# A bias subtraction goes from VectorE to GpSimd, and one first-layer tile takes its low-weight products last

## The chip, the cores and the metric

The kernel runs on one core of one Trainium2 chip. The metric is the device time of one execution in microseconds. The kernel before takes 559.72 us (median of three runs, 559.51 to 559.85). A core has five engines that work side by side and meet through semaphores: TensorE (PE, matrix products), VectorE (DVE), ScalarE (ACT), GpSimd (POOL) and SyncE (SP), which here only issues transfers.

## The reference

The kernel normalises an input of 2048 rows and 512 columns, sends it through a long convolution (a state-space scan, done with Fourier transforms) and, beside that, through a two-layer network whose output gates the convolution:

```python
def _B_ref(x, w1, b1, w2, b2):
    h = jnp.einsum("bsd,df->bsf", x, w1) + b1
    h = _gelu(h)
    return jnp.einsum("bsf,fd->bsd", h, w2) + b2

x = A_u
xn = _layernorm(x, axis=-1)
s = _A_ref(xn, ...)            # convolution of xn with a kernel made from A, B, C
g = _silu(_B_ref(xn, B_w1, B_b1, B_w2, B_b2))
return x + s * g
```

All of it is float32. w1 is 512 x 1792, w2 is 1792 x 512, b2 has 512 entries. The change lies in the two-layer network, at its very beginning.

## The kernel before

**The split into high and low halves.** TensorE multiplies rounded numbers (type fp32r). To keep float32 accuracy every operand is held as two: a high half (the number rounded to fp32r) and a low half (the number less its high half). A product w·x is taken as wh·xh + wh·xl + wl·xh. For the weights, `split(f, k)` makes the four pieces of slice f: w1h and w2h by a cast on ScalarE (L239), w1l and w2l by a subtraction on VectorE or GpSimd (L241). For the input, `ln_high` (ScalarE, L378) and `ln_low` (VectorE, L384) make xh and xl from the transposed, normalised rows. Between the layers, ScalarE makes hf by the gelu (`gate`, L270) and its high half hh (`gate_high`, L276), and VectorE the low half hl (`ffn_rest`, L282).

**Tiles and slices.** The rows are taken in four tiles of 512; the hidden width of 1792 in 14 slices of 128. A step is one pair (v, f) of row tile and slice. In the first layer a step is 12 products of 128x512 into one PSUM bank: four pieces k of the 512 columns, three products each. There are two such banks (tag f1, bufs=2), so the first products of slice f wait until the gelu of slice f-2 has read its bank. `first_start` (L266) makes the first step with all wh·xh, then all wl·xh, then all wh·xl. `first_half(v, f, h)` makes all later steps in two calls, h = 0 for k = 0, 1 and h = 1 for k = 2, 3; its three lines are L256 (wh·xh), L257 (wh·xl) and L258 (wl·xh). `second_part` (L295 to L297, with the bias product of L294) makes the second layer for 128 rows.

**The bias row.** The bias b2 is added by a product too: a 128x512 tile b2r, zero but for row 0 (the high half of b2) and row 32 (the low half), is multiplied by a tile of ones (L294). `bias_load` brings b2 into rows 0 and 32 of a zeroed tile, `bias_high` casts it to b2r on ScalarE (L420), and `bias_low` (L423) then makes row 32 the difference: one instruction on a single partition with 512 columns.

**The order.** Every engine executes its own queue in the order in which the program issues the instructions; the order is written out by hand. `prologue()` comes first: the loads of the first two pairs of input tiles, weights of slices 0 and 1, the time-step arithmetic on GpSimd (L468 to L482), the parameters of the convolution kernel, then

```python
        bias_high()
        ln_stats(0, mv[:, 0:2, :])
        bias_low()
        ln_stats(1, mv[:, 2:4, :])
        split(0, 0)
```

and the normalisation, the transposes and `first_start`. `ln_stats` are the batch statistics on VectorE (L327, L328); the two calls take the first and the second pair of input tiles. After that a list of tokens sets the order. Its start is

```
WS.0.3 LD.0 LD.1 WS.1.0 WS.1.1 P.0 P.0 W.2 G.0 H.0 WB.2 P.0 WS.1.2 P.0 F.1.0 P.0 LS.3.1 LS.2.0 R.0 S.0.0
W.3 WS.2.0 LS.3.0 WS.2.1 LL.4 WS.1.3 LL.5 S.0.1 LS.2.1 WS.2.2 F.1.1 WB.3 F.2.0 ...
```

F.1.0 and F.1.1 are the two calls of `first_half` for step 1, which is (v, f) = (0, 1); S.0.0 and S.0.1 between them are the second layer of step 0 for its first 256 rows; R.0 makes hl of step 0; WS.1.2 makes w1l of slice 1. W and WB load a slice's weights over SyncE's queue into four staging buffers, so the load of slice f waits until slice f-2 has been split. P.0 are pieces of the parameters of the convolution kernel, among them six products on GpSimd (L496 to L501), two absolute values on ScalarE (L504, L505), and a chain on VectorE that starts at L508.

Of the kernel before, what the change touches and what calls it, by code (L numbers as in the profile page):

```python
# [24 lines left out]
KD = D // P  # L25
# [147 lines left out]
def kernel(  # L173
# [5 lines left out]
    V, A, GP, PE, SY = nc.vector, nc.scalar, nc.gpsimd, nc.tensor, nc.sync  # L179
# [69 lines left out]
    def first_half(v, f, h):  # L249
        xh, xl = xt[v]  # L250
        wh, wl, _, _ = W[f]
        if h == 0:
            pt[v, f] = ps1.tile([P, TB * P], F32, tag="f1", name=f"f1_{v}_{f}", bufs=2)
        p = pt[v, f]
        for k in (2 * h, 2 * h + 1):
            PE.matmul(p, wh[:, k, :], xh[:, k, :], start=(k == 0), stop=False)  # L256
            PE.matmul(p, wh[:, k, :], xl[:, k, :], start=False, stop=False)  # L257
            PE.matmul(p, wl[:, k, :], xh[:, k, :], start=False, stop=(k == KD - 1))  # L258
# [42 lines left out]
    SB = {}  # L301
# [118 lines left out]
        A.copy(b2r, SB["b2"])  # L420

    def bias_low():
        V.tensor_sub(b2r[32:33], SB["b2"][32:33], b2r[32:33])  # L423

    def bias_spread():
        SY.dma_start(b2b, b2.rearrange("(o d) -> o d", o=1).to_broadcast([P, D]))
# [242 lines left out]
    b2r = wka.tile([P, D], F32R, name="b2r")  # L669
# [7 lines left out]
    def prologue():  # L677
# [20 lines left out]
# [5 lines that stand above are left out]
# [26 lines left out]
    def skip_load():  # L729
# [3 lines left out]

    acts = {
        "F": lambda j, h: first_half(*steps[j], h),
        "G": lambda j: gate(*steps[j]),
        "H": lambda j: gate_high(*steps[j]),
# [357 lines left out]
    with tc.manual_schedule():  # L1095
# [9 lines left out]
        for p in "S0 F00 S1 S2 F01 S3 L0 F10 L1 A0 F11 A1 L2 L3 A2 A3".split():  # L1105
            if p[0] == "F":
                k = int(p[1]), int(p[2])
# [67 lines left out]
```

## Time and profile before

| | |
|---|---|
| time, median of 3 runs | 559.72 us (559.51 to 559.85) |
| the profiled execution's own time | 559.77 us |
| its span, first to last instruction | 558.0 us |
| TensorE busy | 540.2 us, 97% |
| VectorE busy | 454.2 us, 81% |
| ScalarE busy | 407.8 us, 73% |
| GpSimd busy | 296.3 us, 53% |
| mean granted TensorE clock | 0.998 |

Times in the profile are microseconds from the span's start. In a row of the timeline stand start, length, engine, line, operation, written tile, read tiles, and shapes; a bracket at its end tells how long the engine stood idle before it and what ended that. "PE" is TensorE's products; "SPq" is SyncE issuing a transfer. A row of a table of stretches has the stretch, its length, then the busy time of PE, PEld (weight loads of TensorE), DVE, ACT and POOL with counts, the granted clock, the transfer engines' mean share, and GB/s. Rows that sum up a line give the number, and the shortest, median and longest length in ns.

### The profile page before, as it was taken

Reading aid. Unit: us, or ns where it says so; the run is one execution under the profiler, and the core shown is the slowest. Engines: PE = TensorE matmul, PEld = TensorE weight load, DVE = VectorE, ACT = ScalarE, POOL = GpSimd, SP = SyncE. Lnnn points to the kernel's source line nnn. Section 1 sums busy time; section 2 is a strip of 40 time slices with the busy share of each in tenths; the row PEclk is TensorE's granted clock in tenths of the full one; section 3 lists DMA queues with packets and bytes.
Section 4 is the critical chain, followed back from the end, with each engine's and each line's share of the span. In section 5 each row is a group of like instructions: output and inputs, shape, how many; then the busy total and the mean of one; then the engine's idle time right before and its main releaser. Section 6 shows DMA issues by size and latency. Waiting matters only on the chain.

```text
span 558.0 us, 17143 instructions
## 1 busy us (share of the span) xinstructions
PE 540.2 (97%) x7179; PEld 432.1 (77%) x7179; DVE 454.2 (81%) x697; ACT 407.8 (73%) x602; POOL 296.3 (53%) x403
## 2 busy tenths in 40 slices
PE   8899999999999999999999999999999999999995
PEld 7567777777777777767777777777889998988872
DVE  6899999999997799988988969877357657767874
ACT  3589997977598999668989798995355565564542
POOL 5639585776966769857718747540320305014323
PEclk9999999999999999999999999999999999999999
DMA  8959337267468392426167049205965583615945
GB/s 188 288 161 311 84 96 210 61 210 228 135 189 269 133 295 81 143 75 192 57 188 219 21 114 186 61 11 181 365 245 79 140 128 95 191 46 127 197 120 113
DMA packets 108345, 86.92 MB, mean 156 GB/s; under 512 B 44294, under 2 KB 87562, under 8 KB 108268
## 3 DMA queue, kind: packets, MB, share of 16 engines
q1 hardware_dynamic: 97584, 65.37, 43.8%
q0 software_dynamic: 9568, 19.93, 12.1%
q8 instruction: 56, 0.92, 0.7%
q10 hardware_dynamic: 1116, 0.53, 0.4%
q14 instruction: 21, 0.17, 0.1%
HBM read 52.25 MB, written 33.55 MB: 154 GB/s over the span
## 4 chain that ended last, share of the span: by engine, by line
PE 68%; DVE 16%; issue 6%; DMA 5%; SPq 2%; ACT 1%; POOL 1%; DVEq 0%; POOLq 0%
PE z L295 8%; PE z L296 7%; PE z L297 7%; PE f L256 7%; PE f L258 7%; PE f L257 7%; PE s L883 6%; PE kg L656 5%; PE s L864 4%; PE sa L918 3%; DMA w2s<-in_B_w_dram 2%; PE ph L595 2%; PE w L936 2%; DVE e L641 2%; DVE hl L282 2%
## 5 line engine op out<-in xcount | busy, mean ns | idle before, releaser
L618 POOL TENSOR_TENSOR mm<-mm,rc 128x32 f32<-128x32 f32 (+4 forms) x150 | 110.7, 738 | 11.8
L295 PE MATMUL z<-w2h,hh 128*128 128x512 f32 x224 | 97.9, 437 | 0.0
L256 PE MATMUL f<-xh,w1h 128*128 128x512 f32 x220 | 92.0, 418 | 0.5 <-ACT hf L270 0.5
L297 PE MATMUL z<-w2h,hl 128*128 128x512 f32 x224 | 88.5, 395 | 0.9 <-DVE hl L282 0.9
L296 PE MATMUL z<-w2l,hh 128*128 128x512 f32 x224 | 88.7, 396 | 0.0
L258 PE MATMUL f<-xh,w1l 128*128 128x512 f32 x220 | 86.9, 395 | 1.5 <-DVE w1l L241 1.5
L257 PE MATMUL f<-xl,w1h 128*128 128x512 f32 x220 | 86.7, 394 | 0.0
L883 PE MATMUL s<-X,mc 64*64 64x128 f32 x2048 | 63.5, 272 | 0.9 <-issue 0.9
L900 DVE TENSOR_TENSOR t<-s,uh 128x512 f32<-128x512 f32 x64 | 41.1, 685 | 25.9 <-ACT uh L891 25.6
L883 PEld LDWEIGHTS s<-X,mc 64*64 64x64 f32 x2048 | 56.0, 133 | 4.8 <-issue 2.7
L641 DVE TENSOR_TENSOR e<-mm,ra 128x1024 f32<-128x1024 f32 x32 | 47.8, 1495 | 4.7 <-POOL mm L618 3.2
L297 PEld LDWEIGHTS z<-w2h,hl 128*128 128x128 f32 x224 | 42.1, 188 | 11.7 <-DVE hl L282 1.8
L258 PEld LDWEIGHTS f<-xh,w1l 128*128 128x128 f32 x220 | 41.3, 188 | 11.9 <-DVE w1l L241 2.1
L615 POOL COPY mm<-rc 128x32 f32<-128x32 f32 x30 | 15.4, 512 | 65.4 <-DVE e L648 49.0
L256 PEld LDWEIGHTS f<-xh,w1h 128*128 128x128 f32 x220 | 41.5, 189 | 10.3 <-ACT hf L270 1.2
L282 DVE TENSOR_TENSOR hl<-hf,hh 128x512 fp32r<-128x512 f32 x56 | 46.7, 838 | 3.4 <-ACT hh L276 3.3
L295 PEld LDWEIGHTS z<-w2h,hh 128*128 128x128 f32 x224 | 42.5, 190 | 9.0
L609 DVE SCALAR_TENSOR_TENSOR ra<-ra,ph 128x512 f32<-128x512 f32 x64 | 43.6, 681 | 6.9 <-ACT ra L603 6.0
L296 PEld LDWEIGHTS z<-w2l,hh 128*128 128x128 f32 x224 | 42.3, 189 | 7.9
L257 PEld LDWEIGHTS f<-xl,w1h 128*128 128x128 f32 x220 | 41.4, 188 | 8.9
L870 ACT COPY X<-s 128x512 f32<-128x512 f32 x56 | 28.9, 598 | 25.6 <-PE s L864 25.6
L645 DVE TENSOR_TENSOR e<-mm,ra 128x1024 f32<-128x1024 f32 x32 | 45.6, 1425 | 0.0
(185 smaller groups left out, 1146.2 us busy)
## 6 DMA issues: line engine op xcount, KB each, us to landing
x<-in_A_u_dram SPq DMA_DIRECT2D x16, 256.0 KB
xs<-x SPq DMA_DIRECT2D x16, 256.0 KB
xt_h<-xh POOLq DMA_DIRECT2D x4, 1024.0 KB, 5.4
xt_l<-xl POOLq DMA_DIRECT2D x4, 1024.0 KB, 7.3
kgd<-ko SPq DMA_DIRECT2D x32, 128.0 KB
za<-zo SPq DMA_DIRECT2D x4, 1024.0 KB
xh<-xt_h POOLq DMA_DIRECT2D x4, 1024.0 KB, 6.8
xl<-xt_l POOLq DMA_DIRECT2D x4, 1024.0 KB, 10.1
```

What stands on the lines that cost most here:

```text
L256: PE.matmul(p, wh[:, k, :], xh[:, k, :], start=(k == 0), stop=False)
L257: PE.matmul(p, wh[:, k, :], xl[:, k, :], start=False, stop=False)
L258: PE.matmul(p, wl[:, k, :], xh[:, k, :], start=False, stop=(k == KD - 1))
L282: V.tensor_sub(hl, hf, hh)
L295: PE.matmul(z, hh[:, s], wh, start=(f0 == 0 and not rows), stop=False)
L296: PE.matmul(z, hh[:, s], wl, start=False, stop=False)
L297: PE.matmul(z, hl[:, s], wh, start=False, stop=(f0 == FA - 1))
L609: V.scalar_tensor_tensor(ra[:, 0, c], ra[:, 1, c], MAGIC, p, op0=ALU.subtract, op1=ALU.subtract)
L618: GP.tensor_mul(mv[:, :, 0:3:2, w:2 * w], mv[:, :, 0:3:2, 0:w], rc[:, 2 + 2 * i:4 + 2 * i, :].rearrange("p j c -> p c j").unsqueeze(3).to_ ...
L641: V.tensor_mul(e1, m1.unsqueeze(1).to_broadcast([P, 2, CH, N1]), ra[:, :, :, :N1])
L645: V.tensor_mul(e2[:, :, :, :H], m2[:, :, :H].unsqueeze(1).to_broadcast([P, 2, CH, H]), ra[:, :, :, dn])
L883: PE.matmul(p[ka * 64:(ka + 1) * 64, r, o, :, jj], mc[h, k, ((0, 2), (1, 0))[c][o], :], xf[b][h, c, :, k, :], start=(c == 0), stop=(c == 1 ...
```

## The change

Two edits. `bias_low` is issued on GpSimd's queue instead of VectorE's; there it stands behind the time-step arithmetic and ahead of the six parameter products. And in step (0, 1) `first_half` issues its twelve products in another order: the first call makes the four wh·xh and the four wh·xl, the second the four wl·xh. The number of products and all operands stay the same, as do all other steps.

```diff
@@ def first_half(v, f, h)
         p = pt[v, f]
+        if (v, f) == (0, 1):
+            for w, x in (((wl, xh),) if h else ((wh, xh), (wh, xl))):
+                for k in range(KD):
+                    PE.matmul(p, w[:, k, :], x[:, k, :], start=(w is wh and x is xh and k == 0), stop=(w is wl and k == KD - 1))
+            return
         for k in (2 * h, 2 * h + 1):
             PE.matmul(p, wh[:, k, :], xh[:, k, :], start=(k == 0), stop=False)
@@
     def bias_low():
-        V.tensor_sub(b2r[32:33], SB["b2"][32:33], b2r[32:33])
+        GP.tensor_sub(b2r[32:33], SB["b2"][32:33], b2r[32:33])
```

On TensorE's queue the eight products without w1l now stand before the seven products of S.0.0 and S.0.1, and the four with w1l behind them; before, six stood on either side, two of each six with w1l.

## The prediction

> **What bounds the kernel now.** I read the head of the page first, then the chain of waits over the first 36 us, then the timelines of VectorE, TensorE, GpSimd and ScalarE over the same stretch.
>
> ```profile
> span 558.0 us, 17143 instructions
> PE 540.2 (97%) x7179; PEld 432.1 (77%) x7179; DVE 454.2 (81%) x697; ACT 407.8 (73%) x602; POOL 296.3 (53%) x403
> q8 instruction: 56, 0.92, 0.7%
> ```
>
> TensorE is busy for 97% of the span, so only time in which it stands still, or work taken off it, can be won. The change touches the first 26 us alone. The chain of waits there (start, length, what) is this:
>
> ```profile
> 1.38 4.27 DMA x<-in_A_u_dram
> 7.49 0.43 DVE b2r L423
> ...
> 19.25 5.83 DMA w2s<-in_B_w_dram
> ...
> 26.48 6.76 DMA w2s<-in_B_w_dram
> ...
> 35.04 0.50 PE f L256
> ```
>
> The subtraction that moves (L423) is in the chain. But from 19.25 to 33.24 us the chain is two weight loads with 1.40 us of work between them (25.08 to 26.48). That is the main thing to see: after the two edits come two transfers. The next rows are TensorE's in order of time (start, length; the bracket is what it stood still for).
>
> ```profile
> 18.59 0.40 PE L257 MATMUL f<-xl,w1h 128*128 128x512 f32 x1
> 20.49 0.50 PE L258 MATMUL f<-xh,w1l 128*128 128x512 f32 x1 [1.51 <-DVE w1l L241]
> 22.70 0.51 PE L297 MATMUL z<-w2h,hl 128*128 128x512 f32 x1 [0.30 <-DVE hl L282]
> 25.14 0.39 PE L256 MATMUL f<-xh,w1h 128*128 128x512 f32 x1
> 25.61 0.40 PE L258 MATMUL f<-xh,w1l 128*128 128x512 f32 x1
> 29.69 0.51 PE L256 MATMUL f<-xh,w1h 128*128 128x512 f32 x1
> 34.02 0.50 PE L297 MATMUL z<-w2h,hl 128*128 128x512 f32 x1 [0.57 <-DVE hl L282]
> 35.04 0.50 PE L256 MATMUL f<-xh,w1h 128*128 128x512 f32 x1 [0.52 <-ACT hf L270]
> ```
>
> The two starts at 25.14 and 25.61 are two products apart, so a 128x512 product takes a step of 0.235 us. The wait of 1.51 us in the tile of slice 1 is what the new order goes for.
>
> **The change part by part: GpSimd takes the subtraction.** These are VectorE's rows:
>
> ```profile
> 7.49 0.68 DVE L423 TENSOR_TENSOR b2r<-b2st,b2r 1x512 fp32r<-1x512 f32 x1
> 8.20 0.69 DVE L327 BATCH_NORM_STATS2 bst<-x 128x6 f32<-128x512 f32 x1
> 17.58 0.28 DVE L508 TENSOR_TENSOR pr_ci<-pr_bi,pr_cr 128x128 f32<-128x128 f32 x1
> 19.75 0.68 DVE L241 TENSOR_TENSOR w1l<-w1s,w1h 128x512 fp32r<-128x512 f32 x1
> 21.98 0.66 DVE L282 TENSOR_TENSOR hl<-hf,hh 128x512 fp32r<-128x512 f32 x1
> 24.78 0.67 DVE L241 TENSOR_TENSOR w1l<-w1s,w1h 128x512 fp32r<-128x512 f32 x1
> ```
>
> From 7.49 to the statistics at 8.20 are 0.71 us. Without the subtraction the statistics could begin 0.71 us earlier, if the second pair of input tiles is there. I think it is not:
>
> ```profile
> 0.75 2.48 SPq L322 DMA_DIRECT2D x<-in_A_u_dram  x4
> 5.65:8.00 2.35, 2.35 (x20) 2.35 (x20) 2.15 (x5) 0.48 (x1) 1.75 (x8) 1.00 1.06 234
> ```
>
> Four loads of 256 KB were issued one behind the other, ahead of all weights. In the chain the second landed at 1.38 + 4.27 = 5.65. At 234 GB/s (the last number of the second row) the other two need 0.262 MB / 234 GB/s = 1.12 us each: 7.89 us. So the second pair's statistics begin at about 7.95 and not at 7.49. I take 0.25 us off VectorE's line, not 0.71; the bounds are 0 and 0.71. VectorE runs from there to 17.58 almost without a gap, so the transposes and the first tile come earlier by the same.
>
> On GpSimd the subtraction is queued behind the time-step arithmetic (last row at 11.42) and ahead of the parameter products (first row at 12.49):
>
> ```profile
> 11.42 0.20 POOL L482 TENSOR_TENSOR sm_dt<-sm_e,sm_k 128x4 f32<-128x4 f32 x1
> 12.49 0.68 POOL L496 TENSOR_TENSOR pr_wr<-pr_cr,pr_br 128x128 f32<-128x128 f32 x1 [0.87 <-DMA pr_br<-in_A_B_re_dram]
> 15.29 0.90 POOL L501 TENSOR_TENSOR pr_wi<-pr_wi,pr_m 128x128 f32<-128x128 f32 x1
> 16.55 0.30 ACT L505 ACTIVATE pr_cr<-pr_wi 128x128 f32<-128x128 f32 x1
> L241 POOL TENSOR_TENSOR w2l<-w2s,w2h x4: 1284/1301/1663, 34.5 to 239.8; 128x512 fp32r<-128x512 f32 x4
> L241 POOL TENSOR_TENSOR w1l<-w1s,w1h x2: 1563/1772/1982, 187.6 to 203.3; 128x512 fp32r<-128x512 f32 x2
> ```
>
> No row shows GpSimd on one partition. VectorE's 1x512 took 0.68 us, like its 128x512 of the same kind (0.68 at 19.75), so the time goes by the 512 columns, and GpSimd's 128x512 subtractions of 1.28 to 1.98 us (minimum and maximum of the two rows) are the nearest. I take 1.3 us: 11.7 to 13.0. It first fills the 0.87 us that GpSimd stood idle, and then pushes the six products by 13.0 - 12.49 = 0.5 us (0.3 to 1.2): they end at 16.7 instead of 15.29 + 0.90 = 16.19. Behind them stands ScalarE's absolute value L505 (0.30 us), and behind that VectorE's L508. VectorE now reaches L508 at 17.58 - 0.25 = 17.33, GpSimd and ScalarE are through at 16.7 + 0.30 = 17.0, a few hundredths for the hand-over aside: hidden. The cover is gone if the subtraction takes more than about 1.6 us; at 1.98 us L508 starts at 17.75, 0.17 us later than before. TensorE reads the bias row only after slice 1's products, long after 13.7 us.
>
> On that price the Trainium skill has a rule against the change: SBUF — State Buffer, Who interferes with whom, says that a VectorE instruction with two SBUF inputs and a GpSimd one that reads SBUF shut each other out for a whole instruction. By it the subtraction could wait for one such VectorE instruction of 0.68 us, which gives 1.3 + 0.68 = 1.98 us, the upper bound that the second GpSimd row gives already.
>
> **The new order in the tile of slice 1 (L256 to L258 of that tile alone).** TensorE's work stays the same, 12 products; what moves is which of them need w1l. Before the rows of the second layer (one bias product, then z) stood six products, two of them with w1l; now eight without it. They begin at 18.35 - 0.25 = 18.10 (18.59 less a step, less VectorE's gain), take 8 x 0.235 = 1.9 us, and three more products of the second layer follow: 20.7 us. So the wait of 1.51 us for w1l goes. What is late next is hl, 21.98 + 0.66 on VectorE: with 0.25 off it is 22.4, and TensorE goes on at 22.70 - 0.25 = 22.45. The waits of 1.51 and 0.30 us become one of about 1.75 us. Behind it stand eight products now, not ten, which is 0.47 us. At the end of slice 1 TensorE is ahead by 0.25 + 0.47 = 0.7 us (0.3 to 1.2): it could start slice 2 at 24.42 instead of 25.14.
>
> **What the transfers leave of that.** ScalarE's rows (the bracket is what it waited for):
>
> ```profile
> 23.94 0.62 ACT L239 CAST w1h<-w1s 128x512 fp32r<-128x512 f32 x1 [2.38 <-DMA w1s<-in_B_w_dram]
> 27.02 0.62 ACT L239 CAST w1h<-w1s 128x512 fp32r<-128x512 f32 x1 [1.30 <-DMA w1s<-in_B_w_dram]
> 28.95 0.69 ACT L270 ACTIVATE hf<-f,b1s 128x512 f32<-128x512 f32 x1
> 32.59 0.62 ACT L239 CAST w1h<-w1s 128x512 fp32r<-128x512 f32 x1 [2.29 <-DMA w1s<-in_B_w_dram]
> 25.00:30.00 5.00, 5.00 (x22) 3.69 (x21) 3.35 (x10) 3.54 (x5) 2.59 (x5) 1.00 1.05 232
> 31.00:32.50 1.50, 1.50 (x8) 1.23 (x7) 1.40 (x6) 0.00 (x0) 0.00 (x0) 1.00 0.12 40
> ```
>
> Slice 2's high half is cast at 23.94, when its load lands, and done at 24.56. Its low half follows on VectorE (24.58 to 25.25), so slice 2's third product starts near 25.3 instead of 25.61: 0.3 us are left of 0.7. Slice 3's tile (29.69) needs the bank that the activation at 28.95 frees at 29.64; that stands on ScalarE behind the cast at 27.02, again a load. There 0 is left. The same comes once more at 35.04: the activation that TensorE waits for there (0.52 us, ACT hf) is queued behind the cast at 32.59. The transfer engines' share is 1.05 over 25 to 30 us: they are never idle, so a load asked for a few tenths earlier waits in the same line. Only slice 4's load is asked for earlier, by at most 24.78 - 24.58 = 0.2 us, since VectorE's low half of slice 2 releases its buffer.
>
> The sum, against the profiled execution's own 559.77 us (558.0 and 1.8 around it): 0.7 us at slice 1, 0.3 at slice 2, 0 to 0.2 from 35.04 on. I take 0.1 us. The median of the runs is 559.72, 0.05 below the profiled run, so I forecast 559.6 us. A measurement of this kernel can tell about 0.2%, 1.1 us; this is no difference.
>
> **The rivals.** *The gain stays.* If loads of slices 2 to 4 landed earlier with TensorE, 0.7 us would remain (1.2 at the bound): 559.0, at best 558.5. Against it stands the transfer share of 1.05. It ends inside 0.2% unless all bounds fall together.
>
> *The stragglers go.* From 31.0 to 32.5 us the transfer share is 0.12, two engines of 16, while ScalarE waits for slice 4: one or two engines hold the last parts back. One cause can be seen:
>
> ```profile
> q8 instruction: 1, 0.02, 3.3%
> ```
>
> This is from the DMA queues between 20 and 22 us (packets, MB, share of 16 engines). One packet of queue 8 kept one engine for 0.033 x 16 x 2 us = 1.06 us. The page has 56 such packets, 0.92 MB, which is 64 bytes for each of TensorE's 2 x 7179 instructions: blocks of TensorE's own program. The block came as TensorE went on after its wait, so it should now come about 2 us earlier, at 18 to 19 us. If it then does not hold the weights back, slices 3 and 4 land 1 to 1.5 us sooner, the wait at 35.04 goes, and hl of slice 1 (34.02, less 0.25) decides: about 1.1 us, 558.6.
>
> *The stragglers grow* (the slower side). The same block, now earlier, falls among input loads instead of the result stores, and costs its engine again 1.06 us or more before slices 2 to 4, whose parts stand in that engine's line. From the point where slice 3 lands after 27.0 and slice 4 after 32.6, every microsecond passes through the activations to 29.69 and 35.04: 1.1 to 1.5 us, 560.9 to 561.2. Runtime: NRT & Kernel Launch, Instruction fetch mechanics, in the Trainium skill, calls the cost of such a block mostly hidden; by that neither straggler rival moves the time, and it would be 559.6. The row of 1.06 us on one engine speaks for a cost.
>
> *It doesn't do what it says.* If the second pair of inputs lands after 8.2 us, VectorE gains nothing; only the 0.47 us remain at slice 1, and 0 at 29.69: 559.7, the same forecast.
>
> **How the numbers follow.** The forecast, with the last rival and the gain that stays within 0.2%: 0.60. Stragglers go, or the gain stays in full: 0.21. Stragglers grow, or GpSimd's 1.98 us and they together: 0.19. The likeliest case alone gives 559.0 to 560.1. For 8 in 10 the range reaches to the others' ends: 558.5 to 560.9, which leaves out some of the slower tail.
>
> **What would show it.** In the changed kernel: no wait for w1l in slice 1; one wait for hl of 1.5 to 2.1 us; the second pair's statistics at 7.9 to 8.0; GpSimd's 1x512 of 1.3 us at 11.7; casts of slices 2, 3 and 4 still at 23.9, 27.0 and 32.6 within some tenths; slice 3 at 29.7 and slice 4's tile at 35.0. I am wrong if those casts move by over half a microsecond either way, or if TensorE's start at 35.04 holds and the end still moves.

## The result: slower by half a per cent, and the profile after

| | before | changed |
|---|---|---|
| median of 20 runs each, side by side | 560.25 us (558.77 to 563.27) | 563.72 us (559.66 to 565.34) |
| ratio, 95% interval | | 1.0053 [1.0038, 1.0068] |
| the profiled execution's own time | 559.77 us | 559.66 us |
| its span | 558.0 us | 557.9 us |

The changed kernel is slower by 0.53% (3.5 us between the medians), outside the range and on the other side of no change. One thing has to be known to read its profile: of its 20 runs 19 lie between 561.41 and 565.34 us, and the profiled one, 559.66, is the twentieth. So this profile shows how the loss begins, and not the larger part of what the change costs in most runs. That part was found in a second profile of the same kernel, the first experiment below.

The chain of waits of the changed kernel from its start to 34.6 us (start, length, what), against the chain of before that the prediction shows:

```profile
2.65 5.20 DMA x<-in_A_u_dram
7.95 0.71 DVE bst L332
...
11.36 1.12 DVE rs L352
12.51 2.33 DVE x L357 x4
...
22.82 0.95 POOL pr_h L530
...
28.39 0.35 DVE pr_ci L536
...
33.95 0.68 DVE hl L287
```

The two weight loads that held the chain of before from 19.25 to 33.24 us are gone from it. In their place stand VectorE and, from 20.78 to 28.36, GpSimd with the pieces of the convolution parameters, up to hl of step 1 at 33.95. And the row at 11.36 is a surprise: the last small operation of the inverse root (128x4) is over a microsecond long. The timelines say why. VectorE (DVE), GpSimd (POOL) and TensorE (PE) of the changed kernel, in order of time:

```profile
11.16 0.16 DVE L351 SCALAR_TENSOR_TENSOR t<-t,va 128x4 f32<-128x4 f32 x1
11.20 1.26 POOL L428 TENSOR_TENSOR b2r<-b2st,b2r 1x512 fp32r<-1x512 f32 x1
11.36 1.11 DVE L352 SCALAR_TENSOR_TENSOR rs<-t,rs 128x4 f32<-128x4 f32 x1
...
18.38 0.28 DVE L513 TENSOR_TENSOR pr_ci<-pr_bi,pr_cr 128x128 f32<-128x128 f32 x1
...
22.79 0.66 DVE L287 TENSOR_TENSOR hl<-hf,hh 128x512 fp32r<-128x512 f32 x1
23.50 0.50 PE L302 MATMUL z<-w2h,hl 128*128 128x512 f32 x1 [1.62 <-DVE hl L287]
...
33.95 0.68 DVE L287 TENSOR_TENSOR hl<-hf,hh 128x512 fp32r<-128x512 f32 x1
34.65 1.74 POOL L241 TENSOR_TENSOR w2l<-w2s,w2h 128x512 fp32r<-128x512 f32 x1 [6.15 <-ACT w2h L239]
34.69 0.50 PE L302 MATMUL z<-w2h,hl 128*128 128x512 f32 x1 [0.69 <-DVE hl L287]
35.21 0.50 PE L261 MATMUL f<-xh,w1h 128*128 128x512 f32 x1
...
45.12 0.39 PE L600 MATMUL ph<-cbs,lh 96*128 96x512 bf16 x1 [0.85 <-DVE ra L614]
```

GpSimd's subtraction takes 1.26 us, 11.20 to 12.46. VectorE's operation of the same kind as the one ahead of it (0.16 us) begins at 11.36 and ends at 12.47, with GpSimd's. VectorE stood still for 0.95 us while its row counts as busy. From there VectorE is late: L513 (L508 of before) at 18.38 instead of 17.58, hl of step 0 at 22.79 instead of 21.98, TensorE's z at 23.50 instead of 22.70. At 35.21 only 0.17 us of that is left in this run, but at 45.12 TensorE waits again for VectorE, 0.85 us that the kernel before doesn't have. From there to 400 us TensorE is 1.1 to 1.2 us behind the kernel before, worked out from the starts of its products of the same number in both. It ends 0.1 us ahead: after 400 us, where nothing was changed, this run happened to be faster.

ScalarE's casts of slices 2, 3 and 4 in the changed kernel (the bracket is what it waited for):

```profile
24.02 0.62 ACT L239 CAST w1h<-w1s 128x512 fp32r<-128x512 f32 x1 [1.66 <-DMA w1s<-in_B_w_dram]
27.52 0.62 ACT L239 CAST w1h<-w1s 128x512 fp32r<-128x512 f32 x1 [1.41 <-DMA w1s<-in_B_w_dram]
32.78 0.62 ACT L239 CAST w1h<-w1s 128x512 fp32r<-128x512 f32 x1 [1.99 <-DMA w1s<-in_B_w_dram]
```

They stand 0.08, 0.50 and 0.19 us behind those of before: the loads moved little.

### The profile page after: what moved, and what is told of

Read it like the earlier page. It is cut to its first block, busy times and chain, and to the rows that moved or that the text cites. A ratio compares the mean times of both kernels' runs of the same rounds, so it can differ in the third digit from the quotient of the medians.

```text
span 557.9 us, 17144 instructions
## 1 busy us (share of the span) xinstructions
PE 540.9 (97%) x7179; PEld 432.8 (78%) x7179; DVE 453.9 (81%) x696; ACT 408.0 (73%) x602; POOL 297.6 (53%) x404
## 4 chain that ended last, share of the span: by engine, by line
PE 65%; DVE 21%; issue 5%; DMA 3%; SPq 2%; POOL 2%; ACT 0%; DVEq 0%; POOLq 0%
PE z L300 8%; PE z L301 7%; PE z L302 7%; PE f L261 7%; PE f L263 7%; PE f L262 6%; PE s L888 6%; PE kg L661 5%; PE s L869 4%; PE sa L923 3%; PE ph L600 2%; DVE hl L287 2%; DVE e L646 2%; PE w L941 2%; DVE e L650 1%
## 5 line engine op out<-in xcount | busy, mean ns | idle before, releaser
L261 PE MATMUL f<-xh,w1h 128*128 128x512 f32 x216 | 90.3, 418 | 0.0
L263 PE MATMUL f<-xh,w1l 128*128 128x512 f32 x216 | 85.3, 395 | 0.2 <-DVE w1l L241 0.2
L262 PE MATMUL f<-xl,w1h 128*128 128x512 f32 x216 | 85.1, 394 | 0.0
L646 DVE TENSOR_TENSOR e<-mm,ra 128x1024 f32<-128x1024 f32 x32 | 46.3, 1447 | 4.7 <-POOL mm L623 3.2
L275 ACT ACTIVATE hf<-f,b1s 128x512 f32<-128x512 f32 x56 | 38.6, 690 | 9.8 <-PE f L263 4.6
```

What stands on the lines that cost most here:

```text
L646: V.tensor_mul(e1, m1.unsqueeze(1).to_broadcast([P, 2, CH, N1]), ra[:, :, :, :N1])
```

## The experiments

Three explanations were set against each other. *Collision*: GpSimd's subtraction and VectorE, both reading SBUF, shut each other out, VectorE is late by most of a microsecond, and something later turns that into more. *Order*: the new order of products costs the time, through what TensorE asks for and when. *Lateness*: whatever makes VectorE late at the start is paid again in many places.

**The changed kernel again.** No edit; a second profile, and twelve runs.

> The changed kernel itself, for a second profile and on the same chip as the three below. In its first profile GpSimd's 1x512 subtraction ran from 11.20 to 12.46 us, and VectorE's last step of the inverse root (two inputs in SBUF, 128x4) took 1.11 us from 11.36, where it took 0.16 before: it came to an end as GpSimd did. Theory A (the two engines shut each other out, as the Trainium skill, SBUF - State Buffer, Who interferes with whom, states it): VectorE's first bias-independent row after it, the scaling, starts at 12.4 to 12.6 again, and the low half hl of step 0 at 22.6 to 22.9 instead of 21.98. Time: 1.003 to 1.007 of the kernel before. Theory B (the new order of products, one long wait of TensorE): the same time here.

Median 563.61 us, ratio 1.0045 [1.0022, 1.0068]. This profiled execution is the slowest of its twelve (566.02 us, span 564.2). Its first 13 us are those shown above: L352 takes 1.11 us there too. The difference comes at 34 us. VectorE, GpSimd and TensorE of this run:

```profile
33.68 2.71 POOL L241 TENSOR_TENSOR w2l<-w2s,w2h 128x512 fp32r<-128x512 f32 x2 [4.88 <-ACT w2h L239]
34.02 1.25 DVE L556 CAST pc<-xp 128x256 bf16<-128x256 f32 x1
35.19 1.75 DVE L287 TENSOR_TENSOR hl<-hf,hh 128x512 fp32r<-128x512 f32 x1
...
36.99 0.79 PE L302 MATMUL z<-w2h,hl 128*128 128x512 f32 x1 [2.70 <-DVE hl L287]
```

GpSimd makes the low halves of w2 of slices 3 and 4, one behind the other. VectorE's cast (0.29 us elsewhere) takes 1.25, and hl, for which TensorE waits, 1.75 instead of 0.68. TensorE stands still for 2.70 us and starts this product at 36.99; in before it was 34.02. That is 2.97 us later, where the run shown above lost 0.67. Before, hl was done ahead of GpSimd's pair; these rows of before, from the same view, show it:

```profile
33.28 0.69 DVE L282 TENSOR_TENSOR hl<-hf,hh 128x512 fp32r<-128x512 f32 x1
34.48 2.54 POOL L241 TENSOR_TENSOR w2l<-w2s,w2h 128x512 fp32r<-128x512 f32 x2 [6.64 <-ACT w2h L239]
```

GpSimd's pair starts when ScalarE has cast w2 of slice 3. That cast is queued behind both casts of slice 4, so it goes by slice 4's load: the pair starts anywhere from 33.68 to 35.02 us in the nine profiles in which nothing holds GpSimd back. VectorE begins hl at 32.65 to 33.28 us in the three of them where it is on time, ahead of GpSimd each time; with 0.7 us or more lost its turn comes at 33.95 or later. So the lateness opens the collision, the load decides in each run who is first, and whoever is second waits for a whole instruction.

The table of stretches of this run (stretch, its length, busy time of PE, PEld, DVE, ACT and POOL, granted clock, transfer share, GB/s) and, from its chain of waits, TensorE's steps:

```profile
36.00:38.00 2.00, 1.01 (x2) 0.83 (x3) 2.00 (x3) 0.97 (x2) 0.39 (x1) 0.61 0.61 169
38.00:40.00 2.00, 2.00 (x6) 1.57 (x5) 1.86 (x9) 1.98 (x3) 0.24 (x1) 0.54 0.71 243
```

```profile
37.78 0.43 PE f L261
...
39.49 0.43 PE f L262
39.91 0.26 PE f L263
```

After the stand-still the clock is granted at 0.54 to 0.61, and five products take 0.43 us each instead of 0.235: 0.98 us, and 0.29 more for the first (0.79 instead of 0.50). Of the 6.2 us between this span and that of before, 3.5 are there at 61 us, worked out from the starts of TensorE's products of the same number in both; most of the rest comes after 400 us and is not in the next experiment.

**Only GpSimd's subtraction.** The order of products as before.

```diff
-        V.tensor_sub(b2r[32:33], SB["b2"][32:33], b2r[32:33])
+        GP.tensor_sub(b2r[32:33], SB["b2"][32:33], b2r[32:33])
```

> Only the move to GpSimd; the products of slice 1 in the order of before. Theory A: the same 1.11 us row on VectorE, everything on VectorE 0.8 us late, and TensorE, which has lost the 0.47 us of the other order, starts slice 1's first product with w1l at 21.3 instead of 20.49. Time 1.004 to 1.008. Theory B: 0.999 to 1.001.

563.44 us, 1.0062 [1.0042, 1.0082]: the whole loss. In its timeline both collisions are there:

```profile
11.23 1.26 POOL L423 TENSOR_TENSOR b2r<-b2st,b2r 1x512 fp32r<-1x512 f32 x1
11.30 1.21 DVE L347 SCALAR_TENSOR_TENSOR rs<-t,rs 128x4 f32<-128x4 f32 x1
...
34.07 3.09 POOL L241 TENSOR_TENSOR w2l<-w2s,w2h 128x512 fp32r<-128x512 f32 x2 [5.24 <-ACT w2h L239]
34.26 1.75 DVE L282 TENSOR_TENSOR hl<-hf,hh 128x512 fp32r<-128x512 f32 x1
35.93 1.78 DVE L241 TENSOR_TENSOR w1l<-w1s,w1h 128x512 fp32r<-128x512 f32 x1
```

**Only the order of products.** The branch for (0, 1) of the diff, the subtraction on VectorE.

> Only the new order of products; the subtraction stays on VectorE at 7.5 us. Theory A: VectorE's rows as before (scaling at 11.86, hl at 21.98), TensorE's two waits joined in one of about 2.0 us before 22.70, slice 1 done 0.47 us sooner, nothing left at 29.7. Time 0.998 to 1.001. Theory B: 1.003 to 1.007.

560.94 us, 1.0008 [0.9988, 1.0028]: no difference. TensorE has one wait for hl in the place of two, as the prediction has it (1.62 us; the expectation said about 2.0), and the gain is gone at 35 us:

```profile
22.62 0.50 PE L302 MATMUL z<-w2h,hl 128*128 128x512 f32 x1 [1.62 <-DVE hl L287]
...
35.02 0.50 PE L261 MATMUL f<-xh,w1h 128*128 128x512 f32 x1 [0.71 <-ACT hf L275]
```

The explanation by the order falls with that.

**Both edits, the subtraction earlier on GpSimd.** It goes into the time-step arithmetic, where VectorE has ended one pair of statistics and waits for the next pair of inputs.

```diff
+            bias_low()            # in the time-step loop, first pass, on GpSimd
...
+        bias_high()               # ahead of the time-step arithmetic
...
-        bias_high()
         ln_stats(0, mv[:, 0:2, :])
-        bias_low()
```

> Both edits, but the subtraction stands in the middle of GpSimd's time-step arithmetic, so that it runs at about 7.3 to 8.6 us, while VectorE does batch statistics with one input in SBUF. Theory A: no VectorE row is drawn out, the second statistics start at 7.95, the scaling at 11.6, hl at 21.7; time 0.998 to 1.000. Theory B: 1.003 to 1.007, as with both edits.

559.80 us, 1.0001 [0.9971, 1.0031]. The loss is gone with the same subtraction on the same engine, 3.9 us earlier. VectorE's row is short again:

```profile
7.29 1.26 POOL L428 TENSOR_TENSOR b2r<-b2st,b2r 1x512 fp32r<-1x512 f32 x1
...
11.41 0.16 DVE L352 SCALAR_TENSOR_TENSOR rs<-t,rs 128x4 f32<-128x4 f32 x1
```

**Both edits, and GpSimd held back at 34 us.** GpSimd copies four columns of step 1's hl ahead of the first of the two subtractions, which therefore come behind it. The first collision stays.

```diff
-WS.3.3.1 WS.4.2 LS.5.0 ...
+GD.1 WS.3.3.1 WS.4.2 LS.5.0 ...
+    "GD": lambda j: GP.tensor_copy(gsc, ht[steps[j]][1][:, :4].bitcast(F32)),
```

> Both edits as in the changed kernel, and one more GpSimd instruction (128x4 copied from hl of step 1) ahead of GpSimd's two weight subtractions of slices 3 and 4, so that these can't start before hl of step 1 is made. Theory A2: the first collision (near 11.4 us) only makes VectorE 0.8 us late; the loss comes from a second collision that this lateness opens, near 34 us: GpSimd's 128x512 subtractions (33.68 in the profile with span 564.2) start ahead of VectorE's hl of step 1 (34.2) and hold it back by 1 to 2.7 us, TensorE stands still, and its granted clock falls to 0.54 to 0.61 for some 2 us. Then here: the 1.1 us row at 11.4 is still there, hl of step 1 takes 0.68 us, no dip of the clock at 36 to 42, time 0.999 to 1.002. Rival (the 0.8 us of lateness itself is what is paid for, at many places): 1.003 to 1.006 as without the copy.

561.39 us, 1.0013 [0.9995, 1.0031]. The first collision is unchanged (L352 1.12 us), the second is gone:

```profile
34.23 0.68 DVE L287 TENSOR_TENSOR hl<-hf,hh 128x512 fp32r<-128x512 f32 x1
...
35.53 2.56 POOL L241 TENSOR_TENSOR w2l<-w2s,w2h 128x512 fp32r<-128x512 f32 x2
...
45.58 0.39 PE L600 MATMUL ph<-cbs,lh 96*128 96x512 bf16 x1 [0.94 <-DVE ra L614]
```

Against 1.0045 of the changed kernel (each against the kernel before on its own chip) this takes away about 0.3%, 1.8 us. The two intervals overlap a little; by them the second collision is most of the loss. What is left is not told apart from nothing by its interval; the wait of 0.94 us at 45.58, which before doesn't have, is where the trace shows VectorE's lateness being paid without the second collision. The profile of the result has the same wait (0.85 us at 45.12).

**The early subtraction and the guard together; the guard alone on the kernel before.** The edits of the last two experiments together, and the guard by itself.

> The kernel with GpSimd's bias subtraction early (at 7.3 us), and the same copy ahead of GpSimd's two weight subtractions. Theory A2: neither collision can happen; TensorE's start after the second transfer wait is at 34.3 to 34.6 instead of 35.04; time 0.998 to 0.9995, and fewer long runs than without the copy. Rival (lateness paid at many places): also about 0.999, but no different from the kernel without the copy.

> The kernel before with only the copy from hl of step 1 ahead of GpSimd's two weight subtractions. Theory A2: in the kernel before hl starts 1.2 us ahead of GpSimd, so the copy changes nothing in most runs: 0.998 to 1.000. Rival: the copy itself costs or helps elsewhere, which would show here as well, by over 0.002.

Together: 559.19 us, 0.9966 [0.9948, 0.9984], faster than both kernels, and faster than was expected. The guard alone: 560.34 us, 0.9990 [0.9968, 1.0013], no difference that can be told.

**The early subtraction, and VectorE made late in another way.** Two memsets of 128x512 on VectorE behind the inverse root, 0.48 us each, without any collision at 11 us. They write a tile that is overwritten later.

```diff
+        for _ in range(2):
+            V.memset(b2b, 0.0)
```

> GpSimd's bias subtraction early, so that it collides with nothing, and two VectorE memsets of 128x512 (about 0.95 us together) between the inverse root and the scaling: VectorE as late as in the changed kernel, without GpSimd. Theory A2: the second collision near 34 us comes back, hl of step 1 1.7 us or longer, clock dip, time 1.003 to 1.006. Rival (GpSimd's long instruction does harm in another way than by making VectorE late): about 1.000.

563.97 us, 1.0050 [1.0028, 1.0072]: the loss is back. This separates the cause of the lateness from its price: about a microsecond lost on VectorE at 12 us, by other means, opens the second collision. The dip of the clock that was expected with it didn't come.

```profile
33.82 2.54 POOL L241 TENSOR_TENSOR w2l<-w2s,w2h 128x512 fp32r<-128x512 f32 x2 [5.14 <-ACT w2h L239]
...
35.16 1.74 DVE L287 TENSOR_TENSOR hl<-hf,hh 128x512 fp32r<-128x512 f32 x1
...
36.96 0.50 PE L302 MATMUL z<-w2h,hl 128*128 128x512 f32 x1 [2.77 <-DVE hl L287]
```

The stretches of this run behind that stand-still of 2.77 us:

```profile
36.00:38.00 2.00, 1.04 (x5) 0.87 (x6) 2.00 (x3) 1.00 (x2) 0.36 (x1) 1.00 0.63 152
38.00:40.00 2.00, 2.00 (x10) 1.63 (x9) 1.86 (x9) 1.98 (x3) 0.24 (x1) 1.00 0.73 249
```

The clock stays at 1.00 here. So the dip after the stand-still comes on top in some executions, and is no condition of the loss. The other profiles agree: with the subtraction alone TensorE waits 1.74 and 0.74 us (at 36.06 and 37.77), and the clock is then granted at 0.61 and 0.53 over 38 to 40 and 40 to 42 us; with the reading instruction of the next experiment it waits 1.74 and 0.73 us ahead of the same products, and the clock stays at 1.00.

**What collides, measured by itself.** To the kernel before, with its subtraction on VectorE, one GpSimd instruction is added in the time-step loop: one that reads two SBUF tiles, or two that only write.

```diff
+            if c == 0.5:
+                GP.tensor_sub(b2b, SB["b2"], SB["b2"])    # the reading one
...
+            if c == 0.5:
+                for _ in range(2):
+                    GP.memset(b2b, 0.0)                   # the writing ones
```

> The kernel before, with one additional subtraction of a 128x512 tile on GpSimd at the same place, near 9.5 to 11 us; it reads two SBUF tiles. Theory collision: one of VectorE's small rows with two SBUF inputs near there is drawn out from 0.16 us to 0.9 to 1.2 us and ends with GpSimd's row; rows with one SBUF input are not. Rival (the collision in the changed kernel came from the single-partition access or from the shared bias tile): no VectorE row is drawn out.

> The kernel before, with two additional memsets of a 128x512 tile on GpSimd in the midst of the time-step arithmetic, near 9.5 to 11 us, while VectorE is in its statistics and inverse root. The memsets only write. Theory collision (two engines that both read SBUF through the port they share shut each other out, a rule of the Trainium skill's page SBUF, State Buffer, section Who interferes with whom): no VectorE row between 8.2 and 13 us is over 0.3 us longer than in the kernel before. Rival (any long GpSimd instruction holds VectorE up): one small VectorE row there of 0.5 us or more instead of 0.16 to 0.25.

One run each. The reading one, VectorE and GpSimd:

```profile
9.95 1.04 POOL L480 TENSOR_TENSOR b2b<-b2st 128x512 f32<-128x512 f32 x1
10.01 1.01 DVE L337 TENSOR_SCALAR va<-mv,eps 128x4 f32<-128x4 f32 x1
...
34.26 3.02 POOL L241 TENSOR_TENSOR w2l<-w2s,w2h 128x512 fp32r<-128x512 f32 x2 [5.31 <-ACT w2h L239]
34.38 1.75 DVE L282 TENSOR_TENSOR hl<-hf,hh 128x512 fp32r<-128x512 f32 x1
```

A small VectorE operation (0.23 us in before) lasts to about the end of GpSimd's; at 34 us hl comes behind GpSimd's start, takes 1.75, and TensorE's z product comes 2.17 us later than before (36.19). The run takes 563.86 us, span 562.1. A single run's time would not show a loss, since the 23 runs of before on this chip reach up to 564.13 us; the rows show that one needless GpSimd instruction of 1.04 us in the kernel before brings on both collisions. The expectation missed in one point: the row held up is a TENSOR_SCALAR with one tile as its input, and not one with two.

The writing ones:

```profile
9.81 1.11 POOL L481 MEMSET b2b<- 128x512 f32 x2
9.91 0.45 DVE L337 TENSOR_SCALAR va<-mv,eps 128x4 f32<-128x4 f32 x1
10.39 0.55 DVE L338 TENSOR_SCALAR rs<-va 128x4 int32<-128x4 int32 x1
```

Here the expectation missed, and its rival, that any long GpSimd instruction holds VectorE up, had it right: L338 is 0.38 us longer than before (0.17), L337 0.22 us. Each lasts to about the end of one memset (9.81 + 1.11 / 2 = 10.37, and 10.92). VectorE's rows with two SBUF inputs begin only at 10.98, when the memsets are over, so that a writing GpSimd instruction spares those was not tried. Time 560.85 us, span 559.1; hl of step 1 came ahead of GpSimd's pair there.

**The order of products in the fastest version.** The early subtraction and the guard, with the old order and with the new, on one chip.

> The subtraction on GpSimd early (about 7.3 us), the guard on the weights' low halves of slices 3 and 4, and the order of products of before. It tells what the new order of products is worth in the version that was fastest. Theory collision (the place on GpSimd sets the time, the order of products is worth nothing because the weight loads follow): ratio to before 0.996 to 0.999 as with the new order, the two within 0.002 of each other; TensorE's waits in slice 1 are two again, near 1.3 us for w1l and 0.3 us for hl, and the tile of slice 4 starts near 34.5 us. Theory order (the new order makes part of the gain): ratio 0.999 to 1.001, at least 0.002 above the run with the new order on the same chip.

> The fastest version once more, beside the one with the old order: subtraction on GpSimd at about 7.3 us, guard, new order of products. Theory collision: ratio 0.995 to 0.999, no row of VectorE drawn out near 11 us or by the w2l subtractions near 34 us. If the earlier gain was an accident of single runs: ratio 0.999 to 1.001.

Old order 559.43 us, 0.9974 [0.9957, 0.9992]; new order 559.33 us, 0.9966 [0.9945, 0.9986]. The order is worth nothing that these runs can tell; the early place on GpSimd and the guard carry the gain, which came a second time. Where it lies is open: the profiled spans of the three such runs, 557.8, 558.2 and 557.8, are next to the 558.0 of before, whose profiled time (559.77) is below its median (560.89 on this chip). The profiled run of before is one of its faster ones, so what its other runs lose can't be read from these profiles.

**All profiles side by side.** The place of TensorE at 400 us, against the kernel before and worked out from products of the same number, sorts the other thirteen profiles. Where hl of step 1 was held up at 34 us it is 3.7 to 4.4 us behind (the second profile of the changed kernel, the subtraction alone, the late memsets, the reading instruction). Where VectorE was late and hl still came first it is 1.1 and 1.8 us behind (the profile of the result, the changed kernel with the guard), and 0.6 us with the two writing instructions. Where neither collision is there it is between 0.5 us ahead and 0.4 us behind. From 400 us to the end the same comparison moves by -1.2 to +3.1 us without any regard to these groups (+3.1 with the order alone), so the spans of single profiles can't be compared more closely than that. That the runs without a profile divide in the same way is not shown; only their times fit it.

## Why the prediction was wrong, point by point

- **The step that failed: "The change part by part: GpSimd takes the subtraction."** The price of GpSimd's instruction, 1.3 us, was right (1.26). What was missing is what it does to VectorE. The rule of the Trainium skill was weighed (SBUF — State Buffer, Who interferes with whom), but only with GpSimd as the one that waits; that gave an upper bound of 1.98 us for GpSimd's own end. The price on VectorE was put at nothing. VectorE waited instead, 0.95 us; it had won 0.30 us up to there (11.36 against 11.66) and lost 0.14 us more in the scaling behind it (12.51 to 14.77 against 11.86 to 13.98). The term "I take 0.25 us off VectorE's line" was so 0.80 us on it (18.38 against 17.58). The trace agrees with the Trainium skill's rule, down to the point that the later of the two is shut out for the whole instruction: GpSimd began at 11.20, VectorE's step at 11.36. The other direction could be seen in the profile of before. GpSimd's rows there, while VectorE made the bias row (7.49 to 8.17):

```profile
7.29 0.20 POOL L477 TENSOR_TENSOR sm_e<-sm_e,sm_r 128x4 f32<-128x4 f32 x1
7.58 0.65 POOL L478 TENSOR_SCALAR sm_e<-sm_e 128x4 f32<-128x4 f32 x1
```

  The second is three times as long as its like and ends at 8.23. Read then, it would have pointed to both: that the two engines collide in this kernel, and that a long instruction on the one costs the other.
- **Its place was off by 0.5 us:** 11.20 instead of 11.7. The row of 0.65 us is the reason too: with VectorE's subtraction gone, GpSimd's arithmetic is not held up and ends earlier, inside VectorE's inverse root.
- **"Hidden" by the cover up to L508:** the cover was counted on GpSimd's and ScalarE's queues and was there; the delay did not come through them.
- **"0 is left" at 29.69 and 35.04:** this held for a gain, and the experiment with the order alone shows it (29.76 and 35.02). With the early subtraction and VectorE on time, guard or not and in either order, slice 4's tile starts between 33.82 and 35.07, as the cast of slice 4 comes between 31.26 and 32.62: the load sets it, and the load differs by over a microsecond from run to run. It does not hold for a loss. The loads limit how early TensorE can go on, not how late: slice 3's tile starts at 30.36 in the changed kernel, not at the 29.7 forecast. With VectorE late, the chain goes through its parameter pieces to hl of step 1, and 0.67 us of lateness arrives at the z product of 34.02 unchanged.
- **No rival had the second collision.** The slower rival put the loss on slices 3 and 4 landing late. In the second profile of the changed kernel the loss is there although the casts of slices 3 and 4 come earlier than before, at 26.18 instead of 27.02 and at 31.81 instead of 32.59, which is the prediction's own sign of being wrong:

```profile
31.81 0.62 ACT L239 CAST w1h<-w1s 128x512 fp32r<-128x512 f32 x1 [2.37 <-DMA w1s<-in_B_w_dram]
```

  What decided was GpSimd's pair of subtractions against hl, 2.3 us more (2.97 - 0.67), with the clock's dip on top; the early load, hoped for in the faster rival, is what let GpSimd's pair come first there. The block on queue 8 that both straggler rivals move to 18 to 19 us did not move there: it falls between 20 and 21 us in the profiles before and after, and between 21 and 22 us in the second profile.
- **Right:** the second pair's statistics at 7.95 (7.95); one joined wait for hl of 1.62 us (about 1.75); no wait for w1l in slice 1; the casts at 24.02 and 32.78, with 27.52 at the edge of the half microsecond allowed; slice 4's tile at 35.21. One run in twenty landed at the forecast, 559.66 us for 559.6: the profiled one, in which hl was ahead of GpSimd. That is luck: it was 1.1 us behind at 400 us and made it up where nothing was changed.

On the clock, the Trainium skill (TensorE: Matmul & The Clock Gate, What's actually happening) says that it falls to half after an idle window of about 3.4 us, and that the windows run on by themselves. The waits here were shorter, and of two profiles with nearly the same waits one was followed by the dip and one was not, both for 2.70 and 2.77 us and for 1.74 us with 0.74 or 0.73 behind it; that the place in the window decides would fit, but no run here shows it.

## What to carry to other kernels

Moving work to an idle engine has two prices: its time there, and what it does to the engine it leaves. Look in the profile of before for rows that are several times as long as their like, and see which long instruction of the other engine they end with; place the moved work where that other engine waits anyway. And ask of each queue how much lateness it can take, not only how much lead is used up: here 0.7 us or more was enough to meet the next collision in four of the five profiles that had it and no guard. A one-instruction guard that fixes who goes first took about 0.3% off the changed kernel, while the move by itself, put where it collides with nothing, gained nothing that could be told (1.0001).

## What the runs showed of the hardware that was not expected

- A GpSimd subtraction on one partition, 1x512, takes 1.26 us, like one on 128 partitions (1.28 and up). The prediction took it so without a row that showed it.
- A VectorE operation of 0.16 us lasts 1.11 us behind it, and the profile counts all of that as busy. VectorE's total even falls a little (454.2 to 453.9 us), so the busy shares don't show this loss.
- It is not only operations with two SBUF inputs: a TENSOR_SCALAR of 128x4 (0.23 to 1.01 us) and a cast of 128x256 (0.29 to 1.25 us) were held up by a GpSimd that reads, and TENSOR_SCALARs by one that only writes (0.17 to 0.55). The Trainium skill (SBUF — State Buffer, Who interferes with whom) lists cast and tensor_scalar among the operations that can take the port pair shared with GpSimd; the runs agree. The batch statistics beside GpSimd's early subtraction were not held up (0.69 us at 8.02).
- A stand-still of TensorE of 2.70 us was followed by a granted clock of about half for some 3 us (0.61 and 0.54 over two stretches), one of 2.77 us was not; two waits of 1.74 and 0.74 us were (0.61 and 0.53), two of 1.74 and 0.73 us were not.
